# Decode attention: PV with P as the stationary side (4 key rows x 16 columns) and V moving in 512 columns, the diagonal blocks picked by fp32 transposes and a strided fp32 sum

## The chip, the cores and the metric

The kernel runs on one core of a Trainium2 chip. The metric is device time in microseconds; lower is better. Times are medians of several executions. A ratio is the mean time of one kernel's fast runs over that of the other's fast runs of the same rounds, so it is not quite the ratio of the medians quoted beside it. The span of a profile, taken from one execution, is about 2 us shorter than the time of that execution.

## The reference, cut to what matters

```python
B, D, Hq, Hkv, Sk, Dh = 32, 512, 32, 8, 2048, 128
W = max(256, Sk // 4)                       # 512: only the last 512 keys
q = (x @ wq)  -> [B, Hq, 1, Dh]
k, v = the last W rows of the caches, each KV head shared by 4 query heads
p = softmax(q k^T * Dh**-0.5);  o = p v
out = o.reshape(B, 1, Hq * Dh) @ wo
```

There is one query per sequence. The work is mostly to read 32 x 8 x 512 x 128 keys and as many values in bf16, 67 MB, and the two weight matrices, 8 MB.

## The kernel before: what the change touches

Each engine runs its own program in order and waits for semaphores. A step `v` (32 of them, four to a "quad" `q`) transposes half a K chunk: 32 TensorE transposes into four PSUM banks `t`, of which VectorE evacuates banks 0 to 2 and ScalarE bank 3. Once in four steps the scores of the quad before are made (`k == 0`), then softmax follows (`k == 0` and `k == 1`), and P is transposed (`k == 2`). PV of batch `v - 7` is done in step `v`, and VectorE collects its result.

```python
# TensorE
def transposes(v):
    for t in range(4):
        # waits: K chunk landed; bank t of step v-1 evacuated (dve_T or act_T)
        ... 8 transposes of 128x128 bf16 into KT_ps[:, t]     .then_inc(pe_T[t])
def pv_matmuls(b):                       # V stationary, 16 columns of P moving
    pe.wait_ge(dve_oT, ...)              # the one output bank is collected
    for h in range(2):
        for r in range(NR):              # 16
            pe.matmul(o_bank(b)[:, 16*h:16*h+16], lhsT=V_sb[:, b % NV, h, r, :],
                      rhs=PT_sb[...][:, :, r0:r0 + 4], ...)
for v in range(NVB):
    q, k = divmod(v, 4)
    transposes(v)
    if k == 0 and q >= 1: scores(q - 1)
    if v >= PVLAG:        pv_matmuls(v - PVLAG)      # PVLAG = 7
    if k == 2 and q >= 1: pt_transposes(q - 1)
...                                      # the tail: last scores, P, PV, selection, wo

# VectorE
def ot_evac(b):
    dve.wait_ge(pe_PV, b + 1)
    dve.tensor_copy(oT_sb[:, :, b], o_bank(b)[:, 0:HQ]).then_inc(dve_oT, 1)
for v in range(NVB):
    kt_evac(v, 0)
    if k == 1 and q >= 1: softmax_b(q - 1); p_expand(q - 1, 0)
    kt_evac(v, 1)
    if k == 1 and q >= 1: p_expand(q - 1, 1)
    kt_evac(v, 2)
    if k == 1 and q >= 1: p_expand(q - 1, 2); p_expand(q - 1, 3)
    if k == 0 and q >= 1: softmax_a(q - 1)
    if v >= PVLAG: ot_evac(v - PVLAG)
```

## Time and profile before

| what | value | view |
|---|---|---|
| time | 193.24 us median of 6 (192.86 to 193.94) | times |
| DMA | 90% or more busy in every slice but the first and the last two | page, part 2 |
| K chunks reach TensorE every | 10.2 us, so 20.4 us for a quad | timeline |
| a quad where K is ahead of compute | 15.75 us | timeline |
| all ready but the wo products; last wo part lands | 181.8 us; 188.1 us | timeline |

From the page of the kernel before: the busy tenths of the DMA engines in 40 slices of the span, the granted TensorE clock in tenths, and the chain that ended last by engine.

```profile
span 191.4 us, 5984 instructions
...
PEclk9999999969799987999696969997899999996755
DMA  5999999999999999999999999999999999999960
...
DMA 51%; PE 22%; SPq 18%; DVE 6%; issue 1%; DVEq 0%
```

The DMA stream sets the time. The waits view of the kernel before says it again from TensorE's side; the columns are engine and tile, whom it waited for, us in total, times, and the longest.

```profile
PE KT_ps L244 <- DMA K_sb<-in_k_cache_dram: 27.6, 13, 4.6
...
DVE oT_sb L406 <- PE QO_ps L294: 6.4, 11, 3.3
```

VectorE lost only 6.4 us waiting for a PV to collect. Then the timeline of two steps in the kernel before, TensorE first, then VectorE: start and length in us, and how many instructions are merged.

```profile
145.92 1.95 PE L244 MATMUL KT_ps<-ident,K_sb 128*128 128x128 bf16 x32
147.73 0.96 PE L294 MATMUL QO_ps<-PT_sb,V_sb 128*128 128x16 bf16 x32
148.54 1.95 PE L244 MATMUL KT_ps<-ident,K_sb 128*128 128x128 bf16 x32
...
146.57 1.89 DVE L369 COPY KT_sb<-KT_ps 128x1024 bf16<-128x1024 bf16 x3 [0.50 <-PE KT_ps L244]
148.72 0.30 DVE L406 CAST oT_sb<-QO_ps 128x32 bf16<-128x32 f32 x1 [0.27 <-PE QO_ps L294]
```

The evacuation starts 0.65 us after the transposes (146.57 - 145.92), when the first bank is full. The two run side by side, and a step without scores takes 2.6 us.

### The profile page before, as it was taken

Reading aid. Unit: us, or ns where it says so; the run is one execution under the profiler, and the core shown is the slowest. Engines: PE = TensorE matmul, PEld = TensorE weight load, DVE = VectorE, ACT = ScalarE, POOL = GpSimd, SP = SyncE. Lnnn points to the kernel's source line nnn. Section 1 sums busy time; section 2 is a strip of 40 time slices with the busy share of each in tenths; the row PEclk is TensorE's granted clock in tenths of the full one; section 3 lists DMA queues with packets and bytes.
Section 4 is the critical chain, followed back from the end, with each engine's and each line's share of the span. In section 5 each row is a group of like instructions: output and inputs, shape, how many; then the busy total and the mean of one; then the engine's idle time right before and its main releaser. Section 6 shows DMA issues by size and latency. Waiting matters only on the chain.

```text
span 191.4 us, 5984 instructions
## 1 busy us (share of the span) xinstructions
PE 138.8 (73%) x2724; PEld 118.3 (62%) x2724; DVE 104.2 (54%) x190; ACT 57.5 (30%) x70; POOL 12.0 (6%) x43
## 2 busy tenths in 40 slices
PE   0430989368598849884969579695988987867862
PEld 0330986367567845874569566685578687566751
DVE  0001594965249823983398444983398598383301
ACT  3001253307032612362232503460326334315001
POOL 8403000100010001000010001000100000000000
PEclk9999999969799987999696969997899999996755
DMA  5999999999999999999999999999999999999960
GB/s 199 426 433 425 435 408 423 411 434 406 421 412 414 437 391 438 396 436 400 432 400 433 403 428 414 415 418 416 431 421 412 404 408 402 407 413 405 408 241 17
DMA packets 13369, 75.95 MB, mean 397 GB/s; under 512 B 1504, under 2 KB 1568, under 8 KB 10784
## 3 DMA queue, kind: packets, MB, share of 16 engines
q1 hardware_dynamic: 13296, 75.54, 96.2%
q8 instruction: 21, 0.34, 0.7%
q10 hardware_dynamic: 48, 0.03, 0.2%
q14 instruction: 4, 0.03, 0.0%
HBM read 75.53 MB, written 0.03 MB: 395 GB/s over the span
## 4 chain that ended last, share of the span: by engine, by line
DMA 51%; PE 22%; SPq 18%; DVE 6%; issue 1%; DVEq 0%
DMA K_sb<-in_k_cache_dram 43%; PE KT_ps L244 14%; SPq L151 11%; DMA K_sb<-in_wo_dram 8%; SPq L164 5%; PE S_ps L261 4%; DVE P_ex L392 3%; PE QO_ps L294 3%; SPq L136 1%; SPq L143 1%; PE PT_ps L276 1%; DVE w_sb L369 1%; DVE KT_sb L369 1%; PE KT_ps L343 0%; DVE oT_sb L406 0%
## 5 line engine op out<-in xcount | busy, mean ns | idle before, releaser
L244 PE MATMUL KT_ps<-ident,K_sb 128*128 128x128 bf16 x1024 | 73.2, 238 | 28.3 <-DMA K_sb<-in_k_cache_dram 27.6
L244 PEld LDWEIGHTS KT_ps<-ident,K_sb 128*128 128x128 bf16 x1024 | 67.6, 108 | 30.8 <-DMA K_sb<-in_k_cache_dram 28.9
L369 DVE COPY KT_sb<-KT_ps 128x1024 bf16<-128x1024 bf16 x48 | 31.2, 688 | 18.4 <-PE KT_ps L244 18.2
L369 DVE COPY w_sb<-KT_ps 128x1024 bf16<-128x1024 bf16 x48 | 31.4, 688 | 13.8 <-PE KT_ps L244 13.6
L294 PEld LDWEIGHTS QO_ps<-PT_sb,V_sb 128*128 128x128 bf16 x960 | 26.5, 96 | 12.7 <-DVE oT_sb L406 6.7
L294 PE MATMUL QO_ps<-PT_sb,V_sb 128*128 128x16 bf16 x960 | 28.8, 170 | 7.2 <-DVE oT_sb L406 5.6
L459 ACT ACTIVATE KT_sb<-KT_ps 128x1024 bf16<-128x1024 bf16 x16 | 16.4, 1025 | 39.9 <-PE KT_ps L244 39.9
L459 ACT ACTIVATE w_sb<-KT_ps 128x1024 bf16<-128x1024 bf16 x16 | 16.4, 1028 | 33.9 <-PE KT_ps L244 33.9
L392 DVE TENSOR_SCALAR P_ex<-P_f,recip 32x512 bf16<-32x512 f32 x32 | 25.4, 792 | 1.1
L478 ACT ACTIVATE PT_sb<-PT_ps 128x1024 bf16<-128x1024 bf16 x16 | 15.5, 1021 | 7.6 <-PE PT_ps L276 7.6
L375 DVE TENSOR_REDUCE maxv<-S_ps 128x1 f32<-128x512 f32 x8 | 5.5, 692 | 20.3 <-PE S_ps L261 20.3
L206 POOL COPY QBD<-QT_sb 128x32 bf16<-128x32 bf16 x32 | 6.0, 235 | 125.1 <-PE S_ps L261 116.5
L406 DVE CAST oT_sb<-QO_ps 128x32 bf16<-128x32 f32 x30 | 8.9, 297 | 6.6 <-PE QO_ps L294 6.4
L467 ACT ACTIVATE P_f<-S_ps,negmax 128x512 f32<-128x512 f32 x8 | 5.5, 688 | 20.5 <-DVE negmax L377 20.5
L261 PE MATMUL S_ps<-w_sb,QBD 128*32 128x512 bf16 x128 | 10.7, 484 | 0.5 <-ACT w_sb L459 0.5
L261 PE MATMUL S_ps<-KT_sb,QBD 128*32 128x512 bf16 x128 | 10.2, 464 | 0.0
L276 PE MATMUL PT_ps<-ident,P_ex 128*128 128x128 bf16 x128 | 9.4, 232 | 0.0
L224 PE MATMUL PT_ps<-xT_sb,w_sb 128*128 128x32 bf16 x128 | 4.1, 188 | 6.4 <-DMA w_sb<-in_wq_dram 6.4
L276 PEld LDWEIGHTS PT_ps<-ident,P_ex 128*128 128x128 bf16 x128 | 8.3, 105 | 0.1
L224 PEld LDWEIGHTS PT_ps<-xT_sb,w_sb 128*128 128x128 bf16 x128 | 3.7, 104 | 6.8 <-DMA w_sb<-in_wq_dram 4.6
L261 PEld LDWEIGHTS S_ps<-w_sb,QBD 128*32 128x32 bf16 x128 | 3.5, 108 | 5.8 <-issue 5.8
L343 PE MATMUL KT_ps<-K_sb,o_sel 128*32 128x128 bf16 x128 | 4.5, 309 | 2.9 <-DMA K_sb<-in_wo_dram 1.5
(33 smaller groups left out, 32.3 us busy)
## 6 DMA issues: line engine op xcount, KB each, us to landing
K_sb<-in_k_cache_dram SPq DMA_DIRECT2D x16, 2048.0 KB, 21.9
V_sb<-in_v_cache_dram SPq DMA_DIRECT2D x64, 512.0 KB, 18.8
w_sb<-in_wq_dram SPq DMA_DIRECT2D x4, 1024.0 KB, 8.3
K_sb<-in_wo_dram SPq DMA_DIRECT2D x8, 512.0 KB, 16.0
x_sb<-in_x_dram ACTq DMA_DIRECT2D x1, 32.0 KB, 2.9
out_dram<-out_sb SPq DMA_DIRECT2D x1, 32.0 KB, 1.5
```

Of the source, the lines that this page charges most:

```text
L151: sp.dma_start(V_sb[:, b % NV, h].rearrange("p r d -> p (r d)"), cache_rows(v_cache, b, h)).then_inc(sem_v[b % NV], 16)
L164: sp.dma_start(wo_sb[:, hg].rearrange("p i n -> p (i n)"), wo[hg * 512:(hg + 1) * 512, :].rearrange("(m i) n -> m (i n)", i=4),).then_inc( ...
L224: ins = pe.matmul(PT_ps[:, h // 16, :].bitcast(F32)[:, (h % 16) * 32:(h % 16 + 1) * 32], lhsT=wq_sb[:, kt, h * DH:(h + 1) * DH], rhs=xT_sb ...
L244: ins = pe.matmul(KT_ps[:, t, i * 128:(i + 1) * 128], lhsT=K_sb[:, n % NK, 32 * (v % 2) + 8 * t + i, :], rhs=ident[:, :], start=True, stop ...
L261: ins = pe.matmul(S_ps[32 * c:32 * c + 32, :], lhsT=QBD[:, (4 * q + j) % NQB, g, :], rhs=KT[q % 2][:, :, G * j + g, :], start=(j == 0 and ...
L276: ins = pe.matmul(PT_ps[:, r // 8, (r % 8) * 128:(r % 8 + 1) * 128], lhsT=P_ex[:, r, :, :].rearrange("p s g -> p (s g)"), rhs=ident[:, :], ...
L294: ins = pe.matmul(o_bank(b)[:, 16 * h:16 * h + 16], lhsT=V_sb[:, b % NV, h, r, :], rhs=PT_sb[:, q % 2, r, :].rearrange("p (c n) -> p c n", ...
L369: dve.tensor_copy(KT[q % 2][:, r0:r0 + 8].rearrange("p r a s -> p (r a s)"), KT_ps[:, t, :]).then_inc(dve_T, 1)
L392: dve.tensor_scalar(P_ex[rows, :, :, c], P_f32[rows, :].rearrange("p (r s) -> p r s", r=NR), recip[rows, q:q + 1], None, op0=ALU.mult,).th ...
L406: dve.tensor_copy(oT_sb[:, :, b], o_bank(b)[:, 0:HQ]).then_inc(dve_oT, 1)
L459: act.activation(KT[q % 2][:, r0:r0 + 8].rearrange("p r a s -> p (r a s)"), KT_ps[:, 3, :], ACTF.Copy).then_inc(act_T, 1)
L478: act.activation(PT_sb[:, q % 2, 8 * i:8 * i + 8, :].rearrange("p r n -> p (r n)"), PT_ps[:, i, :], ACTF.Copy,).then_inc(act_PT, 1)
```

## The change

Before, each PV matmul loads 128 columns of V to multiply 16 columns of P. The intent is to turn this round: load 64 columns of P (4 key rows x 16) and let V pass in 512 columns, 8 matmuls a batch instead of 32, in pairs that use the two halves of the array's columns. The result holds 4 x 4 blocks of which only the diagonal ones are wanted. ScalarE copies it to SBUF in fp32, TensorE transposes it (four 128x128 fp32 transposes), and VectorE picks and sums the diagonal blocks with one strided reduce. The O transposes take one of the two PSUM banks of P's transposes, so these now go through one bank in two halves.

```diff
             def pv_matmuls(b):
...
-                pe.wait_ge(dve_oT, b if b <= SELCUT else b - 1)
+                pe.wait_ge(act_O, b if b <= SELCUT else b - 1)
...
+                for i in range(4):
+                    for h in range(2):
                         ins = pe.matmul(
-                            o_bank(b)[:, 16 * h:16 * h + 16],
-                            lhsT=V_sb[:, b % NV, h, r, :],
-                            rhs=PT_sb[...],
+                            o_bank(b)[64 * h:64 * h + 64, :],
+                            lhsT=PT_sb[:, q % 2, 4 * h + j, 4 * i:4 * i + 4, :]...,
+                            rhs=V_sb[:, b % NV, h, 4 * i:4 * i + 4, :]...,
+                            start=(i == 0), stop=(i == 3), tile_position=(0, 64 * h),
                         )
+            def o_transposes(b):
+                pe.wait_ge(act_O, b + 1)
+                pe.wait_ge(dve_oT, b)
+                ... 4 fp32 transposes of O_sb[:, b % 2] into OT_ps      .then_inc(pe_OT, 1)
...
             for v in range(NVB):                                   # TensorE
                 transposes(v)
                 if k == 0 and q >= 1:
                     scores(q - 1)
+                if k == 2 and q >= 1:
+                    pt_transposes(q - 1, 0)
+                if v > PVLAG:
+                    o_transposes(v - PVLAG - 1)
                 if v >= PVLAG:
                     pv_matmuls(v - PVLAG)
                 if k == 2 and q >= 1:
-                    pt_transposes(q - 1)
+                    pt_transposes(q - 1, 1)
...
             def ot_evac(b):                                        # VectorE; its loop is unchanged
-                dve.wait_ge(pe_PV, b + 1)
-                dve.tensor_copy(oT_sb[:, :, b], o_bank(b)[:, 0:HQ]).then_inc(dve_oT, 1)
+                dve.wait_ge(pe_OT, b + 1)
+                dve.tensor_reduce(oT_sb[:, :, b]..., <diagonal blocks of OT_ps>, AX.X, ALU.add)...
...
                 if k == 0 and q >= 1:                              # ScalarE
                     do_exp(q - 1)
                 if k == 2 and q >= 1:
-                    pt_evac(q - 1)
+                    pt_evac(q - 1, 0)
+                if v >= PVLAG:
+                    o_evac(v - PVLAG)                              # O_ps -> O_sb, fp32
+                if k == 2 and q >= 1:
+                    pt_evac(q - 1, 1)
```

## The prediction

> **What bounds it now.** The page shows the DMA engines at 90% or more in every slice but the first and the last two, 397 GB/s over the span; the chain that ended last is 51% DMA and 18% DMA issue. The timeline shows K chunks reaching TensorE every 10.2 us (69.8, 100.4, 131.3 us for chunks 6, 9, 12), so 20.4 us per quad of four batches. TensorE waits 27.6 us for K (waits view). Once K is ahead, compute alone makes a quad in 15.75 us (P transposes at 145.03 and 160.78). At the end everything but the wo products is ready at 181.8, and the last wo part lands at 188.1: a slack of about 3 us, since all 128 wo products take about 3.9 us (30 ns each).
>
> **Costs.** Removed: 32 PV matmuls per batch, 0.81 us in sequence, and the DVE cast, 0.30 us. Added per batch:
> - 8 matmuls of 64x512 in column pairs. Score groups of four 32-column tiles repeat every 0.29 us, so four pairs are an estimated 1.2 us (2 us if the pairs do not overlap). PV gets no cheaper.
> - a 128x512 fp32 ScalarE copy, 0.6 us (the Q copy of that shape took 597 ns); ScalarE 57 to about 78 us, still not full.
> - 4 fp32 transposes. bf16 ones repeat every 57 ns. The Trainium skill, "TensorE: Matmul & The Clock Gate", says transpose mode makes FP32 four times faster (Terms), that fp32 gets no fast weight load, and gives columns/1.2 ns for a load: an estimate of 0.55 us for four; no run here shows it yet.
> - a DVE reduce of 128 elements, about 0.35 us.
>
> **What moves.** This decides it. DVE's evacuation of O(v-7) stands before its K evacuations of v+1, as before. But the O transposes it now waits for stand in TensorE's stream behind the K transposes of v+1, after the scores too where k=0. In-order DVE (strict FIFO by the same page, Part 1) therefore cannot evacuate K of v+1 while TensorE makes it, as it does now. Transposes and evacuations alternate. From one O-transpose start to the next, with trace durations and To for the four transposes: plain step To+3.2; with scores (k=3 to 0) To+5.6; k=0 to 1, where the O copy also stands behind the exp, which stands behind the max, To+4.6; k=1 to 2 (four P expansions, then the P transposes) To+6.4. Sum 19.8+4To = 22 us per quad against 20.4 of DMA. From v=8 compute, not DMA, sets the pace; and the catching up of the last chunks at 15.75 us per quad is lost. Starting at 55.7 us, the last iteration starts its O transposes at about 55.7+113.5+12.7 = 182 (the corresponding PV starts at 163.5 now). The tail adds serial hops (PV, copy, transpose, reduce; P transposes through one bank): about 29 us until the wo products, against 18, then 3.9 and 2.8: span 217.7, time 220.
>
> **Predicted**: 220 us, 207 to 234. Faster by over 2%: 0.02; within 2%: 0.05; slower: 0.93.
>
> **Signs.** DMA tenths fall below 9 in the last third; the chain becomes TensorE, DVE, ScalarE instead of DMA; P transposes are spaced 21 to 24 us; DVE waits long for O transposes, TensorE for K evacuations by DVE, and hardly for K loads; the first K evacuation starts after the O transposes, not 0.65 us after the first K transpose; TensorE idles between.
>
> **What would make it wrong.** fp32 transposes at four passes (To 0.9): about 232. Less busy TensorE losing its clock: higher. If the queue's depth (K lands 22 us after issue) and overlap I don't see hide the alternation, quads stay near 20.4 and only the lost catching-up and the tail cost: 200 to 207.

## The result and the profile after

The changed kernel takes 212.22 us (median of 6, 211.17 to 213.32) against 193.24 us: 1.097 times, with a 95% interval of 1.093 to 1.102.

The page of the changed kernel, the same lines as above:

```profile
span 209.0 us, 4806 instructions
...
PEclk9999999879999999999999999999999999999999
DMA  6999999999999999999999999996899995994000
...
PE 46%; DVE 24%; DMA 18%; ACT 4%; issue 4%; SPq 1%; DVEq 0%; ACTq 0%
```

The DMA engines have gaps in the last third and stop altogether well before the end. The chain that was DMA is now TensorE and VectorE by turns. The waits view of the changed kernel:

```profile
DVE oT_sb L451 <- PE PT_ps L328: 72.6, 32, 6.9
...
PE KT_ps L264 <- DMA K_sb<-in_k_cache_dram: 11.2, 4, 5.0
...
PE PT_ps L328 <- ACT O_sb L538: 8.3, 9, 1.0
...
PE KT_ps L264 <- DVE w_sb L413: 5.2, 7, 0.9
...
PE KT_ps L264 <- DVE KT_sb L413: 4.9, 6, 0.9
```

VectorE now stands still for 72.6 us for the O transposes, once per batch. The last wait of TensorE for K data ends at 49.94 us; from then on it waits mostly for VectorE's evacuations and for ScalarE's copy of O. The timeline of two steps of the changed kernel, TensorE and then VectorE, shows why:

```profile
111.20 1.95 PE L264 MATMUL KT_ps<-ident,K_sb 128*128 128x128 bf16 x32
112.99 0.61 PE L328 MATMUL PT_ps<-ident,O_sb 128*128 128x128 f32 x4
113.53 1.05 PE L313 MATMUL O_ps<-V_sb,PT_sb 128*64 128x512 bf16 x8
114.67 2.17 PE L264 MATMUL KT_ps<-ident,K_sb 128*128 128x128 bf16 x32
...
113.63 0.31 DVE L451 TENSOR_REDUCE oT_sb<-PT_ps 128x32 bf16<-128x128 f32 x1 [1.68 <-PE PT_ps L328]
113.84 1.88 DVE L413 COPY KT_sb<-KT_ps 128x1024 bf16<-128x1024 bf16 x3
```

K is evacuated 2.64 us after its transposes began (113.84 - 111.20), not 0.65 us. VectorE's next instruction in its program is the reduce, which waits for O transposes that TensorE does only after all 32 K transposes of the next step. So TensorE transposes while VectorE waits, and then VectorE evacuates while TensorE, after PV, waits for it. A quad now takes 21.56 us, by the starts of P transposes two quads apart (43.12 us):

```profile
87.20 0.62 PE L297 MATMUL PT_ps<-perm,P_ex 128*128 128x128 bf16 x8 [0.58 <-DVE P_ex L436]
...
130.32 0.62 PE L297 MATMUL PT_ps<-perm,P_ex 128*128 128x128 bf16 x8 [0.59 <-DVE P_ex L436]
```

Where the 17.6 us between the two spans (191.4 and 209.0) came from, read from the timelines; the pieces follow each other, so they add up but for rounding:

| stretch | before | after | difference |
|---|---|---|---|
| start to PV (before) or O transposes (after) of the last step | 163.5 | 177.7 | +14.2 |
| from there to the first wo product (the tail) | 18.3 | 26.8 | +8.5 |
| from there to the end of the wo products; before, they wait for the DMA | 7.0 | 2.0 | -5.0 |
| the rest | 2.6 | 2.6 | 0 |

The groups of the page give the price of the new work itself; the columns are count, busy us, mean ns of one, and the idle time before.

```profile
L313 PE MATMUL O_ps<-V_sb,PT_sb 128*64 128x512 bf16 x240 | 31.6, 385 | 1.1 <-ACT PT_sb L529 1.1
...
L328 PEld LDWEIGHTS PT_ps<-ident,O_sb 128*128 128x128 f32 x128 | 13.4, 140 | 16.7 <-ACT O_sb L538 11.9
...
L538 ACT ACTIVATE O_sb<-O_ps 128x512 f32<-128x512 f32 x30 | 17.9, 596 | 20.4 <-PE O_ps L313 20.4
```

From one start to the next, PV takes 0.98 us a batch, where it took 0.80 to 0.81 us before. The four fp32 transposes start 0.11 us apart, 0.44 us in all. So the change brought TensorE no saving to begin with; but 0.6 us a batch, 20 us in all, could have hidden behind the DMA stream (e5 below tests this).

### The profile page after: what moved, and what is told of

It reads as the page before. It is cut to its first block, busy times and chain, and to the rows that moved or that the text cites. A ratio compares the mean times of both kernels' runs of the same rounds, so it can differ in the third digit from the quotient of the medians.

```text
span 209.0 us, 4806 instructions
## 1 busy us (share of the span) xinstructions
PE 155.2 (74%) x2084; PEld 106.7 (51%) x2084; DVE 102.2 (49%) x190; ACT 75.5 (36%) x102; POOL 13.1 (6%) x47
## 4 chain that ended last, share of the span: by engine, by line
PE 46%; DVE 24%; DMA 18%; ACT 4%; issue 4%; SPq 1%; DVEq 0%; ACTq 0%
DMA K_sb<-in_k_cache_dram 18%; PE KT_ps L264 16%; DVE P_ex L436 9%; PE PT_ps L328 9%; PE S_ps L281 8%; PE O_ps L313 8%; DVE w_sb L413 6%; DVE KT_sb L413 5%; PE PT_ps L297 4%; ACT O_sb L538 2%; DVE maxv L419 2%; PE KT_ps L340 1%; ACT PT_sb L529 1%; PE KT_ps L387 1%; ACT P_f L519 1%
## 5 line engine op out<-in xcount | busy, mean ns | idle before, releaser
L264 PEld LDWEIGHTS KT_ps<-ident,K_sb 128*128 128x128 bf16 x1024 | 60.3, 100 | 36.4 <-DMA K_sb<-in_k_cache_dram 12.1
L451 DVE TENSOR_REDUCE oT_sb<-PT_ps 128x32 bf16<-128x128 f32 x32 | 9.8, 306 | 72.6 <-PE PT_ps L328 72.6
L313 PE MATMUL O_ps<-V_sb,PT_sb 128*64 128x512 bf16 x240 | 31.6, 385 | 1.1 <-ACT PT_sb L529 1.1
L328 PE MATMUL PT_ps<-ident,O_sb 128*128 128x128 f32 x128 | 20.4, 282 | 8.8 <-ACT O_sb L538 8.3
L436 DVE TENSOR_SCALAR P_ex<-P_f,recip 32x512 bf16<-32x512 f32 x32 | 25.3, 791 | 1.1
L538 ACT ACTIVATE O_sb<-O_ps 128x512 f32<-128x512 f32 x30 | 17.9, 596 | 20.4 <-PE O_ps L313 20.4
L328 PEld LDWEIGHTS PT_ps<-ident,O_sb 128*128 128x128 f32 x128 | 13.4, 140 | 16.7 <-ACT O_sb L538 11.9
L313 PEld LDWEIGHTS O_ps<-V_sb,PT_sb 128*64 128x64 bf16 x240 | 11.0, 109 | 12.2 <-issue 4.7
L297 PE MATMUL PT_ps<-perm,P_ex 128*128 128x128 bf16 x128 | 10.4, 226 | 5.9 <-DVE P_ex L436 3.5
L297 PEld LDWEIGHTS PT_ps<-perm,P_ex 128*128 128x128 bf16 x128 | 7.6, 101 | 9.9 <-ACT PT_sb L529 5.3
L244 PE MATMUL PT_ps<-o_sel,w_sb 128*128 128x32 bf16 x128 | 4.1, 188 | 5.6 <-DMA w_sb<-in_wq_dram 5.6
```

Of the source, the lines that this page charges most:

```text
L244: ins = pe.matmul(PT_ps[:, h // 16, :].bitcast(F32)[:, (h % 16) * 32:(h % 16 + 1) * 32], lhsT=wq_sb[:, kt, h * DH:(h + 1) * DH], rhs=xT_sb ...
L264: ins = pe.matmul(KT_ps[:, t, i * 128:(i + 1) * 128], lhsT=K_sb[:, n % NK, 32 * (v % 2) + 8 * t + i, :], rhs=ident[:, :], start=True, stop ...
L297: ins = pe.matmul(PT_ps[:, 0, (r % 8) * 128:(r % 8 + 1) * 128], lhsT=P_ex[:, r, :, :].rearrange("p s g -> p (s g)"), rhs=perm[:, :, :], st ...
L313: ins = pe.matmul(o_bank(b)[64 * h:64 * h + 64, :], lhsT=PT_sb[:, q % 2, 4 * h + j, 4 * i:4 * i + 4, :].rearrange("p r n -> p (r n)"), rhs ...
L328: ins = pe.matmul(OT_ps[:, 128 * i:128 * i + 128], lhsT=O_sb[:, b % 2, 128 * i:128 * i + 128], rhs=ident32[:, :], start=True, stop=True, i ...
L436: dve.tensor_scalar(P_ex[rows, :, :, c], P_f32[rows, :].rearrange("p (r s) -> p r s", r=NR), recip[rows, q:q + 1], None, op0=ALU.mult,).th ...
```

## The experiments

Theory A: the cost comes from the order. VectorE's program, left as it was, now waits for something that stands behind the next K transposes, and this takes away the overlap of transposes and evacuations. Theory B: the cost is the added work on TensorE, ScalarE and VectorE. The first four kernels ran on one chip (before: 192.97 us there), the last four on another (192.98 us). All eight gave the right result.

### e1: VectorE collects one batch later, nothing else

```diff
-                if v >= PVLAG:
-                    ot_evac(v - PVLAG)
+                if v > PVLAG:
+                    ot_evac(v - PVLAG - 1)
+            ot_evac(NVB - PVLAG - 1)
             softmax_a(NQUAD - 1)
```

> The changed kernel with one order changed: VectorE collects batch v-8 (not v-7) at the end of step v, so it no longer waits for O transposes that stand behind the next step's K transposes. No work is added or removed. Theory A (the order is the cause): K transposes and their evacuations overlap again, a compute-bound quad would take about 18 us, so the quads fall back to the DMA pace of 20.4 us (P transposes 20 to 20.6 us apart), only the longer tail and slower catching-up stay: 198 to 202 us. Theory B (the added work itself, TensorE, ScalarE and VectorE time, is the cause): quads stay near 21.5 us and the time stays at 210 to 213 us.

Measured: 197.84 us, 1.026 times before (1.022 to 1.029), just under the range of theory A. All the new work is still there. VectorE's wait for the O transposes fell from 72.6 to 16.1 us:

```profile
DVE oT_sb L451 <- PE PT_ps L328: 16.1, 8, 5.3
```

The timeline of one step of e1, TensorE and VectorE:

```profile
145.38 1.95 PE L264 MATMUL KT_ps<-ident,K_sb 128*128 128x128 bf16 x32
...
146.02 1.89 DVE L413 COPY KT_sb<-KT_ps 128x1024 bf16<-128x1024 bf16 x3 [1.12 <-PE KT_ps L264]
```

The evacuation starts 0.64 us after the transposes again, as it did before the change. The DMA tenths of e1's page are full in every slice but the first and the last three, so the stream sets the pace of the quads again. By the starts of the P transposes (61.26 and 142.73 us, four quads apart) a quad takes 20.4 us on average, though single ones range from 18.9 to 22.5 us where 20 to 20.6 had been expected:

```profile
DMA  6999999999999999999999999999999999999500
```

Moving one call in VectorE's program took back 14.4 us of the 19.0 (212.22 - 197.84, in different rounds). Theory B is out as the main cause: the added work without the stale wait does not slow the quads. What it costs together with the wait is taken up after e2.

### e2: the kernel before, with the late order alone

```diff
-                if v >= PVLAG:
-                    pv_matmuls(v - PVLAG)
+                if v > PVLAG:
+                    pv_matmuls(v - PVLAG - 1)
...
-            for b in range(NVB - PVLAG, SELCUT):
+            for b in range(NVB - PVLAG - 1, SELCUT):
```

> The kernel before, with its old PV, cast and transposes, but PV of batch v-8 (not v-7) issued in step v, so that VectorE, whose order is kept, waits for a PV that stands behind the next step's K transposes: the new order with none of the new work. Theory A: K transposes and evacuations alternate; steps of about 4.0, 6.4, 4.0 and 6.1 us make a quad of about 20.5 us where K no longer waits for DMA, the catching-up at the end is lost, about 197 to 201 us. Theory B: the same work gives the same time, 193 to 194 us.

Measured: 206.21 us, 1.069 times before (1.067 to 1.071). The order alone, with the old work, cost 13.2 us in these runs. The direction is theory A's; its size was underestimated by 5 us. The waits view of e2 shows the same signature as the changed kernel's, now with the old cast and the old PV:

```profile
DVE oT_sb L406 <- PE QO_ps L294: 67.2, 29, 8.4
```

and the P transposes of e2 are 20.9 and 21.2 us apart:

```profile
109.62 1.05 PE L276 MATMUL PT_ps<-ident,P_ex 128*128 128x128 bf16 x16
130.54 1.87 PE L276 MATMUL PT_ps<-ident,P_ex 128*128 128x128 bf16 x16
151.75 1.80 PE L276 MATMUL PT_ps<-ident,P_ex 128*128 128x128 bf16 x16
```

The miss is for the most part the clock, which I had not counted. Where the granted clock was 1.00, the four steps between the PV starts at 103.12, 108.82, 112.77, 119.21 and 123.17 us are 5.70, 3.95, 6.44 and 3.96 us: a quad of 20.05 us, less than the 20.5 expected. From 57.66 to 176.10 us there are 22 steps. They took 118.4 us, 8.5 us more than the same steps at full clock (109.9), and all of this excess lies in steps with a stretch of half clock. The lines above show it: two show 1.8 and 1.9 us for 16 transposes that take 1.05 us in the first; at the one of 1.80 us the granted clock was 0.50 (150 to 152 us) and 0.67 (152 to 154 us). At full clock the wait for K data, which comes every 20.4 us a quad, would have taken back a part of the 8.5 us. The wo products took 3.6 us, where they take 1.97 us at full clock in the changed kernel.

This also says what the order does alone. At full clock the alternating steps of the old work make a quad of 20.05 us, just under the 20.4 us of the DMA; the added work without the stale wait stays at 20.4 us (e1); the two together make 21.56 us. So in the quads each is hidden behind the DMA without the other, and the 13.2 us of e2 are the lost catching-up, a tail of 21.6 us where I had assumed 18.3, and time at half clock. The kernel before had as low a clock (0.90 on average, 0.89 in e2), but there the DMA stream set the pace. No run shows e2 at full clock throughout.

### e3: ScalarE copies O before it does the exp

```diff
-                if k == 0 and q >= 1:
-                    do_exp(q - 1)
                 if k == 2 and q >= 1:
                     pt_evac(q - 1, 0)
                 if v >= PVLAG:
                     o_evac(v - PVLAG)
+                if k == 0 and q >= 1:
+                    do_exp(q - 1)
```

> The changed kernel with ScalarE doing the O copy before the exp in the step with scores. Theory A: the step from k=0 to k=1, now 4.85 us, falls to about 3.7 us, the quad from 21.56 to about 20.4 us, five to six quads of it: 204 to 207 us. Theory B (total work): no work is removed, 211 to 213 us.

Measured: 204.16 us, 1.059 times before (1.054 to 1.064), in theory A's range. The P transposes of e3 are 20.33 us apart (105.55, 125.88 and 146.22 us), where about 20.4 had been expected. The O copy behind the exp was the second hop that lengthened the chain, in the one step of four that has it. Again no work was removed.

### e4 and e5: the fp32 transposes twice, in either order

```diff
-                for i in range(4):
+                for i in (0, 1, 2, 3) * 2:
                     ins = pe.matmul(
                         OT_ps[:, 128 * i:128 * i + 128],
```

e4 does this to the changed kernel, e5 to e1.

> The changed kernel with each group of four fp32 transposes run twice (the second writes the same values again; right result). Theory A: the transposes are on the chain of every step, so the quad grows by 4 x 0.44 = 1.8 us to 23.3 us and the tail by eight groups: 212 + 10 + 3 = 223 to 227 us. If they were hidden (as in a kernel bound by DMA), 212 to 214 us. That TensorE time counts here doesn't tell A from B by itself: the same doubling in the order of e1 will.

> e1 with each group of fp32 transposes run twice, as e4 did to the changed kernel. Theory A (the order made the work visible): in e1's order a compute-bound quad took 17.8 us (P transposes at 142.73 and 160.56); 4 x 0.44 more is 19.6 us, still under the DMA pace of 20.4, so the quads up to the last two stay at 20 to 20.6 us and only the catching-up at the end (six steps, 2.6 us) and the tail (eight groups, 3.5 us) grow: 201 to 205 us, 4 to 7 us over e1, against the 16 us that the same doubling cost in the changed kernel's order. Theory B (TensorE work sets the time): as there, 16 us over e1, about 213 us.

Measured: e4 takes 228.27 us, 16 us over the changed kernel and a little over its range. Its quads average 23.9 us, from the second halves of the P transposes at 69.29 and 188.81 us, five quads apart; 23.3 had been expected. This excess is the clock again: the quad from 117.06 to 140.37 us, where the granted clock was full, takes 23.31 us, and the three of 24.1 to 24.3 us each hold 3.4 us at half clock. Together these three are 2.7 us over 23.31 each, more than e4's 1.3 us over its range. e5 takes 203.09 us, 5.3 us over e1 and within its range. The P transposes of e5, the first and the last of four:

```profile
81.72 0.62 PE L297 MATMUL PT_ps<-perm,P_ex 128*128 128x128 bf16 x8 [0.31 <-DVE P_ex L436]
...
143.33 0.62 PE L297 MATMUL PT_ps<-perm,P_ex 128*128 128x128 bf16 x8 [0.30 <-DVE P_ex L436]
```

Over these three quads the mean is 20.5 us, the pace of the DMA, although each step has 0.44 us more of TensorE work. The same work costs 16 us in the one order and 5 us in the other, and in the latter it shows only at the end: against e1's trace, e5's last O transposes of the main loop start 2.2 us later (166.95 and 164.79 us) and its tail is 3.9 us longer (29.4 and 25.5 us).

### e6: both orders mended

This is e1 with e3's edit.

> e1 with e3's order on ScalarE too (O copy before the exp). Theory A: the 8 us that e3 saved came off the step from k=0 to k=1, which is off the chain once VectorE's order is mended: at most 1 us faster than e1, 196.5 to 198.5 us. Rival: ScalarE's queueing is a cost of its own, which adds to that of the order: 190 to 194 us.

Measured: 197.33 us (197.28 to 200.18), where e1 took 197.84 us. e3's edit saved 8 us from the changed kernel and here about half a microsecond, less than e1's own runs differ (197.12 to 198.44 us). The two are hops of one chain, not two costs; with the first mended, the second is hidden behind the DMA.

### e7 and e8: the tail

e1 still lost 4.9 us. Its timeline has the last step's O transposes at 164.79 us, only 1.3 us later than the PV of the kernel before (163.48), and the first wo product at 190.24 us: a tail of 25.5 us against 18.3 us (the 25.3 us below counts from 164.95, where the chain that ended last takes them up). e7 is e1 with the end rearranged, e8 adds e6's order.

```diff
+        def pt_bank(q, i):                 # second half of the last P into a free bank
+            return KT_ps[:, 3, :] if q == NQUAD - 1 and i == 1 else PT_ps[:, 0, :]
...
                 pv_matmuls(b)
+            pe.wait_ge(act_T, NVB)
+            pt_transposes(NQUAD - 1, 0)
+            pt_transposes(NQUAD - 1, 1)
             o_transposes(SELCUT - 1)
...                                         # then the selection
-            pt_transposes(NQUAD - 1, 0)
-            pt_transposes(NQUAD - 1, 1)
...                                         # VectorE
             for c in range(G4):
                 p_expand(NQUAD - 1, c)
-                if NVB - PVLAG + 1 + c < SELCUT:
-                    ot_evac(NVB - PVLAG + 1 + c)
+            for b in range(NVB - PVLAG + 1, SELCUT):
+                ot_evac(b)
...                                         # ScalarE: pt_evac of the last quad before o_sel
```

> e1 with the end rearranged: the last quad's P transposes before the selection and the second half of them into a free bank, all four P expansions before the last two O collections. Theory A: what e1 still loses to the kernel before is the longer serial tail (25.3 us from the last iteration's O transposes to the wo products, against 18.3); this takes about 2.9 us out, so 194 to 196 us. Rival: the rest is lost in the DMA stream before the tail, no change from 197.8 us.

> e7 with e6's order too, the best version of the changed kernel that these findings give. Theory A: the DMA stream of the kernel before is a floor that nothing here lowers, so 193 to 195.5 us and not under 192.5 us. Rival: if PV with V moving had a gain of its own, it would show here as less than the 193 us of before by over 1 us.

Measured: e7 takes 194.06 us (193.95 to 194.13), 1.0055 times before (1.004 to 1.007); e8 takes 194.44 us (194.32 to 195.72), 1.009 times (1.007 to 1.011). Both are within their ranges. e7's first wo product starts at 187.49 us, 2.75 us earlier than e1's; the timelines of e1, e7 and e8 differ in how fast the products then run:

```profile
190.24 3.52 PE L387 MATMUL KT_ps<-K_sb,o_sel 128*32 128x128 bf16 x128 [0.38 <-DVE o_sel L490]
```

```profile
187.49 1.97 PE L392 MATMUL KT_ps<-K_sb,o_sel 128*32 128x128 bf16 x128 [0.38 <-DVE o_sel L495]
```

```profile
187.53 3.52 PE L392 MATMUL KT_ps<-K_sb,o_sel 128*32 128x128 bf16 x128 [0.38 <-DVE o_sel L495]
```

The first is e1, the second e7, the third e8. In e8's profiled execution the granted clock was 0.50 from 188 to 190 us, in e7's it was 1.00. So e8's profile does not show that its order is worse, and this profile was the slowest of e8's runs. The same holds for e1: its profile was taken at 198.44 us, while two of its four runs took 197.1 to 197.3 us, so of the 3.8 us from e1 to e7 only the 2.75 us before the first product are shown to be the order of the tail. Neither version beats the kernel before. With the order mended, the new PV has no gain of its own to show, because the DMA stream is the floor of both kernels.

## Why the prediction was right

The time, 212.22 us, lies in the range of 207 to 234, and 8 us under the point value of 220.

- "In-order DVE (strict FIFO by the same page, Part 1) therefore cannot evacuate K of v+1 while TensorE makes it": shown by the timeline (2.64 us from transposes to evacuation, 0.65 us before), and by e1 and e2, which move this order alone, in both directions. The Trainium skill, "TensorE: Matmul & The Clock Gate", Part 1, says that ScalarE and VectorE queues are strict first-in first-out. The trace agrees: in 32 collections VectorE stood 72.6 us, and the next K evacuations, which are behind these in its program, did not overtake them.
- The sum of steps, 19.8 + 4To: right once To has its measured value; that it agrees to the last digit is luck. With To = 0.44 it gives 21.56 us, and the quads are 21.56 us apart. The four steps by O-transpose starts (102.53, 109.22, 112.99, 119.17, 124.09 us) are 6.69, 3.77, 6.18 and 4.92; the terms predicted 6.84, 3.64, 6.04 and 5.04 with that To. So the single terms were off by up to 0.15 us and the errors cancelled.
- To was mis-sized: 0.55 us estimated, 0.44 measured. The skill's rule on the same page (Part 2, LDWEIGHTS: columns over 1.2 in ns) gives an estimate of 107 ns for 128 columns; the transposes start 110 ns apart (0.44 us over four), so a load each is all they seem to cost, and the extra that I added for the fp32 passes was not there. Whether it is the load or the pass that sets the 110 ns was not tested. e4's quad at full clock agrees with 0.44: 23.31 - 21.56 is 1.75 us for four more groups. The 0.11 us too much in To make 2.5 us over 23 steps. The start of the chain was 1.5 us early as well, 54.2 us and not 55.7. Together they are 4.0 of the 4.3 us by which the last step came before the predicted 182 us. The same page (Terms) says that transpose mode makes FP32 four times faster; an fp32 transpose cost 1.9 times a bf16 one here, and no run shows an fp32 matmul outside transpose mode to compare.
- PV was put at 1.2 us and takes 0.98 us. It lies on the chain (8% of the span by the page), but in the plain step shown above it ends almost together with VectorE's evacuation of the first bank (114.58 and 114.52 us), for which the next K transposes wait as well.
- The tail of "about 29 us" measured 26.8 us. To is in it eight times, which explains 0.9 us; the cheaper PV explains part of the rest.
- The wo products, "3.9", took 2.0 us. I had taken the 30 ns spacing from the kernel before, where the clock was low at that point (tenths of 7, 5 and 5 in the last slices); here it was full. What the products cost at full and at half clock is also seen in e7 and e8, 1.97 and 3.52 us.
- Of the signs, all appeared: gaps in the DMA tenths of the last third, the changed chain, quads between 21 and 24 us, the two waits, and no waits for K loads after 49.94 us. Of the doubts, "Less busy TensorE losing its clock" did not come true: the granted clock was 0.99 on average in the profiled run, against 0.90 before. That rise was not foreseen; in e2, whose steps alternate too, the clock was 0.89.

By the experiments, of the 19.0 us lost, mending VectorE's order takes back 14.4 with the new work in place (e1). Rearranging the tail takes back 3.8 more (197.84 to 194.06), of which 2.75 is shown to be order and the rest may be the clock, and about 1 us is left (e7 to before). These are differences of medians from different rounds, so each may be off by some tenths of a microsecond. They are not the costs of two separate things: the stale wait costs as much as it does because the added work stands on the chain that it makes (the three quads compared at the end of e2).

## What to carry to other kernels

When a producer is moved later in one engine's program, look at every in-order engine that consumes it and ask what stands behind that wait: here one stale wait on VectorE turned two overlapping stages into alternating ones, and mending it took back 14.4 of 19.0 us while every added instruction stayed. In this kernel, bound by DMA, some 0.6 us a step of extra work on other engines was free as long as the steps still overlapped, and the tail after the last load was where it showed. Sum the chain step by step with durations from the trace, program order included; busy shares would have shown little here (TensorE 73% before, 74% after).

## What the Trainium skill lacked or had wrong

- "TensorE: Matmul & The Clock Gate", Part 4, has times for bf16 transposes only. An fp32 transpose of 128x128 started every 110 ns here, a bf16 one every 57 ns (32 in 1.8 us). So fp32 costs 1.9 times bf16 in a row, and each LDWEIGHTS record is 140 ns long.
- The same part says that the full clock does not engage for transpose mode. Here runs of bf16 transposes went at 57 ns each wherever the granted clock was full (1.95 us for 32), and at about 0.11 us where it was half (1.87 us for 16, in e2).
- The same page gives measured speedups for packed 32-wide column tiles and no figure for pairs of 64-wide ones. Eight 64x512 matmuls in four pairs took 0.98 us here; the two of a pair start within 3 ns and the pairs 0.22 to 0.24 us apart. For comparison, "TensorEngine Tiling (Array Packing)", Performance Considerations, warns that tiling speeds up TensorE and not the PSUM evacuation. Here the copy of each result took ScalarE another 0.6 us; no run has the same matmuls untiled to compare.
- "TensorE: Matmul & The Clock Gate", Part 1, ties the loss of the full clock to one window of about 3.4 us in which TensorE is idle, and says of one kernel that frequent short idles between groups of matmuls cost it too, without a measure. In e2 the grant fell to 0.50 at 150 us although no single idle stretch of TensorE in the 8 us before was longer than 1.1 us (it was busy for 1.7 of the last 4 us), and in e8 it fell at 188 us after idle stretches of 0.5 us at most. What share of busy time keeps the full clock was not tested.
